# Conversions of a weight matrix spread over more blocks, a search begun later, and another search counted tile by tile

## The chip, the cores and the metric

The kernel runs on one core of a Trainium2 chip. The metric is the device time of one execution, in microseconds (us); the number given for a kernel is the median of its runs. The core has TensorE (PE; its weight loads are listed apart as PEld), VectorE (DVE), ScalarE (ACT), GpSimd (POOL) and SyncE (SP), which only starts transfers. Each engine works through its own queue in order, and so an instruction that waits holds up all that stands behind it on its engine.

## The reference

Three stages, all in float32. First attention over 4 batches of 8 heads with 576 rows and 64 columns a head, causal, with a bias from running sums of `s`. Its result, 2304 rows (tokens) of 512, goes to a layer of eight experts. Each token may go to one expert and each expert takes 288 tokens: all 2304 x 8 logits are sorted, and from the greatest down a token is given to an expert if it has none yet and the expert isn't full.

```python
order = np.argsort(-flat)
for idx in order:
    tok, e = (int(idx) // E, int(idx) % E)
    if assigned[tok] >= 0 or counts[e] >= cap:
        continue
    assigned[tok] = e
```

Each expert computes `relu(x @ w1[e]) @ w2[e]` with 1024 inner columns. The last stage is `(relu(x @ w_in) ** 2) @ w_out` with 2048 inner columns.

## The kernel before

**Attention first, then blocks.** The attention of all heads takes the first 230 us or so. The rest is `experts` (from line 945). Its matrix work is a list of 288 blocks, `order`, which I number from 0. A block is twelve matmuls (L1065 to L1067 through `mm3`, L1113 to L1115), since each product is made of three, high part by high part and the two mixed ones. A block has a kind: 1 and 2 are the first and second layer of an expert (288 columns a matmul), 3 and 4 are the third and fourth, `w_in` and `w_out`, for the tokens of two experts together (512 columns). Experts 0 and 1 have blocks 0 to 31 (kinds 1 and 2) and then 32 to 63 (kinds 3 and 4, mixed); experts 2 and 3 blocks 64 to 95 and 96 to 127; experts 4 and 5 blocks 128 to 159 and 160 to 191; expert 6 has 192 to 239, expert 7 has 240 to 287.

**The search.** The sort is replaced by eight searches (`route_phases`, L602), one for each place in the order in which experts fill up, place 0 to 7. A search needs the one before it. It finds the 288th largest key by six rounds of counting (two halves of three): VectorE compares all 20 tiles of keys with 42 thresholds (`compare`, L573, into the tile `wide`), TensorE counts the hits, VectorE turns the counts into flags, and TensorE broadcasts the result (L706, L715). The counts are made in one of two ways. For places below `GP` they are made tile by tile, 20 matmuls of 42 columns of weights (L684). For the others three tiles go together: 7 matmuls with 128 columns (L690), a copy to SBUF (L694), 3 selecting matmuls (L697). After the rounds come the position sums (L738, L739), four comparisons that make rows of slots (L763) with 2 x 10 matmuls (L770), and the list of indices (L774). With that list GpSimd gathers the expert's 288 rows from memory by three indirect transfers (L1023), and TensorE transposes them (`xt`; L1039 for expert 0, else L1032).

**How the search is spread.** `route_phases` is a generator; each `yield` ends a piece and gives a number for how long the piece's result takes: 1 for the keys and 1 for the best expert, in each round 2 after the comparison, 0.55 after the grouped count and 1 after the flags (in the tiled way 2 and 1), then 2, 1, 1, 1, 1. That is 29.3 for a grouped search. A counter, `wait[0]`, goes down by the cost of every block (1.0 for kinds 1 and 2; for kinds 3 and 4 1.7 with two experts or with expert 7, 0.9 with expert 6 alone). When it is at or under zero after a block, the next piece is emitted behind that block, and the counter goes up by the piece's number times a factor (`YS` = 0.5 for places 0 and 1, `YL` = 1.3 later; L1363). While fewer than two lists are done, a second look is taken in the middle of a block of kind 1 or 2 (`mid`, L1334). `RF` pieces of the search of place 1 are emitted before block 0, and then the transposes of expert 0's rows.

**What forces it.** Weights are loaded five blocks ahead (`LD`). When the loader reaches the first block of an expert it calls `need` (L1283), and this emits all pieces that are left until that expert's list is there, in one go, ahead of the block in hand. An expert that is the second of its pair is gathered at once and its transposes stand behind the last block of kind 1 of the expert before it (two of four) and the block after that (L1376); for the others the gathers are spread and the transposes follow some blocks later. For expert 1 the transposes stand behind blocks 12 and 13, for expert 3 behind 76 and 77, for expert 5 behind 140 and 141.

**The conversions.** `w_in` and `w_out` come as 64-bit floats and are converted piece by piece (`Convert`, L823), 32 pieces. The 16 of `w_out` are done in attention, two of `w_in` during the search of place 0, and 14 are left when block 0 begins. One `step` is: split a finished piece into high and low part (`store`; ScalarE, then GpSimd L993), finish a piece (`end`, VectorE L888), begin another (`begin` and `begin2`; ScalarE L862 and two VectorE operations, L877), and load one. Before, a step stands behind every second block (`CVM` = 2) from block 18 (`CV0`); and in the blocks of kind 3 of the first pair a loop takes care that the piece a block needs is there (L1082). VectorE also makes the low parts of many other splits (L993, L1143, L1160), squares for the third layer (L1179) and all of the search.

Of the kernel before, what the change touches and what calls it, by code (L numbers as in the profile page):

```python
# [471 lines left out]
NTOK, DM, E_, F1, F2 = 2304, 512, 8, 1024, 2048  # L472
# [3 lines left out]
KT, STEPS, GT = 42, (1681, 41, 1), 3  # L476
NG = (NT + GT - 1) // GT
F16, I16 = mybir.dt.float16, mybir.dt.int16
GP = 1
GY = 0.55  # L480
R0 = [0, 10, 15, 20]
RN = [0, 20]
# [119 lines left out]
def route_phases(tc, cn, L, rp, rps, eids, idxs):  # L602


    nc = tc.nc
# [15 lines left out]
    for ph in range(E_):  # L621
# [8 lines left out]
        else:  # L630
# [8 lines left out]
            khi, klo, wm, oh, cmp = fr.khi, fr.klo, fr.wm, fr.oh, fr.cmp  # L639
            key, base = khi, None  # L640
            for half in range(2):
                for n in range(3):
# [38 lines left out]
                    mi = rps.tile([128, 512], FT, name="mi")  # L681
                    if ph < GP:
                        for t in range(NT):
                            nc.tensor.matmul(mi[:KT, :8], cmp[:, KT * t:KT * t + KT], oh[:, t, :], start=t == 0,  # L684
                                             stop=t == NT - 1)
                    else:

                        for t in range(NG):
                            c0 = GT * KT * t
                            nc.tensor.matmul(mi[:, 128:128 + 8 * GT], cmp[:, c0:c0 + 128],  # L690
                                             oh[:, GT * t:GT * t + GT, :].rearrange("p t e -> p (t e)"), start=t == 0,
                                             stop=t == NG - 1)
                        ev = rp.tile([128, 8 * GT], F16, name="ev")
                        V.tensor_copy(ev, mi[:, 128:128 + 8 * GT])  # L694
                        yield GY
                        for t in range(GT):
                            nc.tensor.matmul(mi[:KT, :8], cn.sel[:, t, :], ev[:, 8 * t:8 * t + 8], start=t == 0,  # L697
                                             stop=t == GT - 1)
# [61 lines left out]
        n = NT // 4  # L760
# [28 lines left out]
NB1, NB2 = F1 // 128, F2 // 128  # L789
# [7 lines left out]
RS = 1  # L797
SD = 6
OD = 1
CVM = 2  # L800
XP = 4
XS = 'GGGS'
XN = [2, 2, 2, 2, 2, 3, 1, 2]
YS = 0.5
GD = 1
GS = 2
YL = 1.3
ML = 3
RF = 8
GE = 2  # L810
ME = 8
SL = 3
# [2 lines left out]
RB = 3  # L815
RL = 1
CVO = 0
CV0 = 18
WU = 10
TE = 8  # L820

# [123 lines left out]
def experts(tc, cn, L, xd, w1, w2, win, wout, out):  # L945
    nc = tc.nc
# [58 lines left out]
    def route_step():  # L1005
        l0 = len(idxs)
        y = next(route, 0)

        return y
# [59 lines left out]
    def block(blk, mid=lambda: None):  # L1069
# [9 lines left out]
            post.append((post1, (e, f, h)))  # L1079
        elif k == 3:  # L1080
            if e == 0:
                while conv.done < NB2 + f + 1:  # L1082
                    conv_step()
                conv.store(win_put)
            yh, yl = Y[e]
            n = 128 * len(GI[e])
            h = ps.tile([128, 512], FT, name="h", bufs=2)
            if len(CHUNKS[e]) == 2:

                o, yh, yl = h.rearrange("p (a n) -> p a n", a=2), *(  # L1090
                    y.rearrange("p d (a n) -> p d a n", a=2)[:, :, :, :256] for y in (yh, yl))
            else:
                o, yh, yl = h[:, :n], yh[:, :, :n], yl[:, :, :n]
            if f == 0 and len(CHUNKS[e]) == 2:

                for a in range(2):
                    for d in range(4):
                        mm3(o[:, a], winH[:, d, 0:128], winL[:, d, 0:128], yh[:, d, a], yl[:, d, a], d == 0, d == 3)
                post.append((post3, (e, f, h)))
                return  # L1100
            for d in range(4):
                mm3(o, winH[:, d, 128 * f:128 * f + 128], winL[:, d, 128 * f:128 * f + 128], yh[:, d], yl[:, d],
                    d == 0, d == 3)
            post.append((post3, (e, f, h)))
        elif k == 4:

            wh, wl = (w.rearrange("p c d -> p (c d)") for w in W.pop(blk))
            hi, lo = ST.pop((e, f))
            if f == 0:
                ACC[k, e] = [ps.tile([128, 512], FT, name=f"acc{g}") for g in range(len(GI[e]))]  # L1110
            for g, o in enumerate(ACC[k, e]):
                c0 = 128 * g
                T.matmul(o, hi[:, c0:c0 + 128], wh, start=f == 0, stop=False)  # L1113
                T.matmul(o, hi[:, c0:c0 + 128], wl, start=False, stop=False)  # L1114
                T.matmul(o, lo[:, c0:c0 + 128], wh, start=False, stop=f == NB2 - 1)  # L1115
            if f == NB2 - 1:
                post.append((post4, (e, ACC.pop((k, e)))))
        else:
            wh, wl = W.pop(blk)
            hi, lo = HT.pop((e, f))  # L1120
            last = NB1 - 1
            if f == 0:
                ACC[k, e] = [ps.tile([128, 512], FT, name=f"acc{d}") for d in range(4)]
            a = ACC[k, e]
            for d in range(4):
                mm3(a[d][:, :CAP], wh[:, d, :], wl[:, d, :], hi, lo, f == 0, f == last)
                if d == 1:
                    mid()
            if f == last:
                post.append((post2, (e, a)))  # L1130
# [209 lines left out]
    for n, blk in enumerate(order):  # L1340
# [19 lines left out]
        turn = blk[0] == 2 and blk[2] == NB1 - 1 and (blk[1] < TE or len(idxs) == E_)  # L1360
        if turn:
            flush()
        if len(idxs) < E_ and wait[0] <= 0 and n >= RS:  # L1363
            wait[0] += route_step() * (YL if len(idxs) > 1 else YS)
            routed = True
        flush()
        if conv.done < 2 * NB2 and n % CVM == CVO and n >= CV0:
# [66 lines left out]
```

## Time and profile before

| | us |
|---|---|
| median of 3 runs | 965.94 (963.07 to 967.32) |
| the profiled execution | 963.51 |
| its span, first to last instruction | 961.7 |
| PE busy | 898.0 (93%) |
| DVE busy | 575.1 (60%) |
| ACT busy | 455.8 (47%) |
| POOL busy | 405.7 (42%) |

The profile is of one execution. Busy time of PE is modelled, as matmuls are pipelined, and so pace is best read from the starts of matmuls. "Granted clock" is TensorE's clock as a share of 2.4 GHz; 0.50 is its lower level, 1.2 GHz. A bracket behind an instruction gives how long its engine was idle before it and what released it.

### The profile page before, as it was taken

To read this page: it belongs to the slowest core of one execution; us is meant where nothing else is said; L and a number is where in the kernel's file an instruction comes from. 1 tells how busy PE (TensorE), PEld (TensorE's weight loads), DVE (VectorE), ACT (ScalarE), POOL (GpSimd) and SP (SyncE) were. 2 spreads that over 40 slices of the span, in tenths; PEclk is the share of its full clock that TensorE was granted. 3 is DMA by queue.
4 is the path that set the end of the run, shared out by engine and by line. 5 is a ranking of instruction groups with operands and counts; after the bars stand their busy time and mean duration, and the time that the engine had idled before them with its cause. 6 is when DMAs were issued, how large, how long until landed. Compare 5 with 4: busy or idle time off the path is not lost.

```text
span 961.7 us, 16567 instructions
## 1 busy us (share of the span) xinstructions
PE 898.0 (93%) x5836; PEld 733.9 (76%) x5836; DVE 575.1 (60%) x1517; ACT 455.8 (47%) x1055; POOL 405.7 (42%) x330
## 2 busy tenths in 40 slices
PE   4999999998688798999999999989999999999996
PEld 3676767776478786777898777889888899898885
DVE  7787888887867988734756444756432344442222
ACT  6677767775334554233353233443432455553321
POOL 4454554443523656646442321633323454533233
PEclk9999999999589999999999999999999999999999
DMA  6877696733634632101641100455000160140001
GB/s 169 212 175 191 152 241 169 189 96 124 202 104 136 204 103 77 33 1 45 208 133 44 33 1 1 136 150 164 13 1 1 49 204 1 29 137 1 0 1 45
DMA packets 73971, 95.54 MB, mean 99 GB/s; under 512 B 8128, under 2 KB 53184, under 8 KB 73888
## 3 DMA queue, kind: packets, MB, share of 16 engines
q1 hardware_dynamic: 68560, 79.93, 30.4%
q0 software_dynamic: 3360, 11.01, 3.4%
q10 hardware_dynamic: 1968, 3.54, 1.0%
q8 instruction: 46, 0.75, 0.3%
q14 instruction: 37, 0.30, 0.1%
HBM read 80.31 MB, written 9.44 MB: 93 GB/s over the span
## 4 chain that ended last, share of the span: by engine, by line
PE 74%; DVE 14%; issue 4%; DMA 4%; POOL 2%; ACT 2%; SPq 0%; DVEq 0%; POOLq 0%; ACTq 0%
PE h L1065 10%; PE h L1067 9%; PE h L1066 9%; PE acc L1113 6%; PE acc L1114 6%; PE acc L1115 6%; PE av L271 5%; PE pt L244 5%; PE acc L1065 3%; PE acc L1067 3%; PE acc L1066 3%; PE sc L199 3%; DVE sg L877 2%; DVE Q L168 2%; PE sc L200 2%
## 5 line engine op out<-in xcount | busy, mean ns | idle before, releaser
L1180 POOL TENSOR_TENSOR sL<-s,sH 128x512 fp32r<-128x512 f32 (+1 forms) x80 | 111.6, 1394 | 252.0 <-DVE s L1179 245.3
L1175 ACT ACTIVATE s<-h 128x512 f32<-128x512 f32 (+1 forms) x80 | 44.5, 556 | 220.7 <-PE h L1067 220.6
L1179 DVE TENSOR_TENSOR s<-s 128x512 f32<-128x512 f32 (+1 forms) x80 | 53.3, 667 | 153.0 <-ACT sH L1178 152.8
L993 POOL TENSOR_TENSOR wL<-raw,wH 128x512 fp32r<-128x512 f32 x64 | 83.5, 1312 | 98.4 <-ACT wH L990 96.2
L1065 PE MATMUL h<-yH,winH 128*128 128x512 f32 (+1 forms) x332 | 124.1, 374 | 0.0
L1067 PE MATMUL h<-yH,winL 128*128 128x512 f32 (+1 forms) x332 | 121.2, 365 | 0.0
L1066 PE MATMUL h<-yL,winH 128*128 128x512 f32 (+1 forms) x332 | 121.0, 364 | 0.0
L1113 PE MATMUL acc<-wH,sH 128*128 128x512 f32 x288 | 116.3, 404 | 0.0
L990 ACT ACTIVATE wH<-raw 128x512 fp32r<-128x512 f32 x128 | 80.2, 629 | 76.0 <-DMA raw<-in_w 39.8
L1114 PE MATMUL acc<-wL,sH 128*128 128x512 f32 x288 | 113.5, 394 | 0.0
L1115 PE MATMUL acc<-wH,sL 128*128 128x512 f32 x288 | 113.5, 394 | 0.0
L227 ACT ACTIVATE e<-sc,nm 128x576 f32<-128x576 f32 (+4 forms) x160 | 84.1, 526 | 48.1 <-DVE junk L216 41.4
L216 DVE TENSOR_SCALAR_CACHE_REDUCE junk<-sc 128x576 bf16<-128x576 f32 (+4 forms) x160 | 77.6, 485 | 34.0 <-PE sc L202 25.7
L244 PE MATMUL pt<-ident,e 128*128 128x128 f32 x448 | 81.4, 288 | 5.3 <-ACT e L227 4.8
L199 PE MATMUL sc<-K,Q 128*128 128x288 f32 (+2 forms) x192 | 74.0, 390 | 10.5 <-DVE Q L152 10.5
L1065 PE MATMUL h<-xH,wH 128*128 128x288 f32 x256 | 81.0, 316 | 2.7 <-DVE hL L1143 2.7
L1065 PE MATMUL acc<-hH,wH 128*128 128x288 f32 x256 | 79.1, 309 | 0.0
L1066 PE MATMUL h<-xL,wH 128*128 128x288 f32 x256 | 77.0, 301 | 0.0
L1067 PE MATMUL h<-xH,wL 128*128 128x288 f32 x256 | 76.4, 299 | 0.1
L1067 PE MATMUL acc<-hH,wL 128*128 128x288 f32 x256 | 75.8, 296 | 0.0
L1066 PE MATMUL acc<-hL,wH 128*128 128x288 f32 x256 | 75.7, 296 | 0.0
L160 POOL TENSOR_TENSOR K<-k,K 64x1152 fp32r<-64x1152 f32 x15 | 39.7, 2648 | 78.8 <-DMA q<-in_qT 21.9
(225 smaller groups left out, 2107.4 us busy)
## 6 DMA issues: line engine op xcount, KB each, us to landing
raw<-in_w SPq DMA_DIRECT2D x128, 256.0 KB
k<-in_kT SPq DMA_DIRECT2D x30, 288.0 KB
q<-in_qT SPq DMA_DIRECT2D x30, 288.0 KB
r<-in_wout SPq DMA_DIRECT2D x16, 512.0 KB
r<-in_win SPq DMA_DIRECT2D x16, 512.0 KB
vb<-in_vm SPq DMA_DIRECT2D x16, 256.0 KB
Q<-Q SPq DMA_DIRECT2D x8, 288.0 KB
QB<-Q SPq DMA_DIRECT2D x7, 288.0 KB
```

Of the source, the lines that this page charges most:

```text
L199: nc.tensor.matmul(o, Q1[:, a, c0:c0 + 128], K1[:, a, x0:x1], start=True, stop=False)
L227: nc.scalar.activation(o, v, AF.Exp, bias=nm[:m], scale=0.125, accum_out=sums[b % 2][:m, i, hd % H:hd % H + 1])
L244: nc.tensor.transpose(pt[:, j, :m], (E4[hd % 2] if i == 4 else E[i])[:m, 128 * j:128 * j + 128], cn.ident[:m, :m])
L990: S.activation(hi, src, AF.Copy)
L993: (G if eng[1] == "G" else V).tensor_tensor(lo, src, f32(hi), op=OP.subtract)
L1065: T.matmul(o, wh, xh, start=first, stop=False)
L1066: T.matmul(o, wh, xl, start=False, stop=False)
L1067: T.matmul(o, wl, xh, start=False, stop=last)
L1113: T.matmul(o, hi[:, c0:c0 + 128], wh, start=f == 0, stop=False)
L1114: T.matmul(o, hi[:, c0:c0 + 128], wl, start=False, stop=False)
L1115: T.matmul(o, lo[:, c0:c0 + 128], wh, start=False, stop=f == NB2 - 1)
L1180: G.tensor_tensor(lo, s, f32(hi), op=OP.subtract)
```

## The change

Six edits. The matmuls that count tile by tile take 128 columns of weights instead of 42 (only the first 42 rows of the result are read), and the search of place 1 is now counted in that way too (`GP` = 2). `RF` goes from 8 to 3. Conversion steps stand behind every fourth block from block 8 instead of every second from block 18, and the loop in the third layer's blocks asks for one piece more than the block needs. The factor of the counter is now a list by the number of lists done (`YY`), read before the piece instead of after it; `mid` keeps `YS`. The search of place 2 isn't begun before block 20 (`R2`). And the counter isn't let below -1.0 when a piece is emitted.

```diff
-GP = 1
+GP = 2
...
-                            nc.tensor.matmul(mi[:KT, :8], cmp[:, KT * t:KT * t + KT], oh[:, t, :], start=t == 0,
+                            nc.tensor.matmul(mi[:, :8], cmp[:, KT * t:KT * t + 128], oh[:, t, :], start=t == 0,
                                              stop=t == NT - 1)
...
-CVM = 2
+CVM = 4
...
-YL = 1.3
+YY = [0, 0.45, 1.2, 1.0, 1.5, 1.5, 1.5, 1.5]
+R2 = 20
 ML = 3
-RF = 8
+RF = 3
...
-CV0 = 18
+CV0 = 8
...
-                while conv.done < NB2 + f + 1:
+                while conv.done < min(2 * NB2, NB2 + f + 2):
                     conv_step()
...
-        if len(idxs) < E_ and wait[0] <= 0 and n >= RS:
-            wait[0] += route_step() * (YL if len(idxs) > 1 else YS)
+        if len(idxs) < E_ and wait[0] <= 0 and n >= (R2 if len(idxs) == 2 else RS):
+            y = YY[len(idxs)]
+            wait[0] = max(wait[0], -1.0) + route_step() * y
```

## Rows read from the trace of the kernel before

**Rows 1.** The page: busy time, share and instructions of PE; its busy tenths in 40 slices of 24 us; the granted clock in the same slices.

```profile
PE 898.0 (93%) x5836; PEld 733.9 (76%) x5836; DVE 575.1 (60%) x1517; ACT 455.8 (47%) x1055; POOL 405.7 (42%) x330
...
PE   4999999998688798999999999989999999999996
...
PEclk9999999999589999999999999999999999999999
```

**Rows 2.** What PE waited for, over the whole span: us in total, times, longest.

```profile
PE mi L697 <- DVE ev L694: 8.3, 7, 3.5
PE mi L690 <- DVE wide L573: 7.6, 6, 2.6
...
PE mi L770 <- DVE wide L763: 4.4, 4, 2.3
...
PE mi L1032 <- DMA rows<-xd,idx: 1.4, 1, 1.4
```

**Rows 3.** Busy time of each engine between block borders: length, busy us (instructions) of PE, PEld, DVE, ACT, POOL, then granted clock, share of the DMA engines, GB/s.

```profile
269.50:289.20 19.70, 18.13 (x142) 15.64 (x142) 14.07 (x45) 7.92 (x17) 6.17 (x5) 0.96 0.37 109
289.20:306.20 17.00, 13.81 (x109) 12.96 (x107) 13.46 (x43) 5.50 (x12) 5.41 (x6) 0.90 0.47 139
306.20:346.50 40.30, 33.97 (x262) 32.14 (x260) 36.11 (x74) 23.41 (x46) 20.82 (x15) 0.96 0.56 169
346.50:397.30 50.80, 45.71 (x245) 35.27 (x245) 45.79 (x83) 23.25 (x41) 34.44 (x24) 1.00 0.23 69
397.30:451.30 54.00, 54.00 (x282) 40.41 (x278) 18.60 (x50) 17.85 (x33) 30.56 (x29) 1.00 0.07 20
```

**Rows 4.** The same columns for three stretches: blocks 192 to 200 and 174 to 185, with no search in between, and blocks 58 to 63, with a search step behind each.

```profile
766.00:780.40 14.40, 14.40 (x110) 14.37 (x109) 6.37 (x10) 7.00 (x14) 11.09 (x13) 1.00 0.76 230
715.70:749.30 33.60, 33.60 (x146) 27.11 (x145) 7.80 (x13) 10.53 (x18) 9.68 (x7) 1.00 0.00 1
...
432.60:451.30 18.70, 18.70 (x96) 13.90 (x96) 4.92 (x14) 6.49 (x11) 12.08 (x15) 1.00 0.11 29
```

**Rows 5.** The chain of waits from 250 to 275 us: start, us, what. The last tiled count of the search of place 0, its last broadcast and its index list; then a grouped count of the next search, its selection, and the transposes of expert 0's rows.

```profile
250.73 0.91 PE mi L684 x20
...
251.87 0.18 PE mi L715
...
257.52 0.16 DVE idx L774
...
266.01 0.38 PE mi L690 x7
...
266.65 0.24 PE mi L697 x3
266.89 2.13 PE acc L1039 x9
```

**Rows 6.** GpSimd's first and third gather for expert 0 (start, us, instruction), and, of all gathers, the time from issue to landing.

```profile
257.98 1.15 POOL L1023 DMA_INDIRECT rows<-xd,idx  x1 [2.11 <-DVE nt L780]
...
260.70 0.96 POOL L1023 DMA_INDIRECT rows<-xd,idx  x1 [0.30 <-issue]
...
DMA to landing us min/median/max: 3.3/3.9/4.7
```

**Rows 7.** The chain of waits from 295 to 304 us: expert 1's index list, the last of its gathers, and the transposes that waited for it.

```profile
295.80 0.17 DVE idx L774
...
298.78 4.68 DMA rows<-xd,idx
...
303.50 0.55 PE mi L1032 x3
```

**Rows 8.** VectorE's time on the conversions in two stretches: length, busy us (instructions), then the columns as before; first the two operations that begin a piece (L877), then the one that ends it (L888).

```profile
306.20:346.50 40.30, 10.64 (x14) 0.96 0.56 169
346.50:397.30 50.80, 16.15 (x12) 1.00 0.23 69
...
306.20:346.50 40.30, 6.95 (x7) 0.96 0.56 169
346.50:397.30 50.80, 5.89 (x7) 1.00 0.23 69
```

**Rows 9.** Weight loads of the tiled count (42 columns) and of the grouped count (128 columns): ns least, middle and most, first and last start, shape.

```profile
L684 PEld LDWEIGHTS <-wide x120: 97/123/131, 232.4 to 251.4; 128*42 128x42 bf16 x120
...
L690 PEld LDWEIGHTS <-wide x252: 95/96/118, 261.4 to 652.0; 128*128 128x128 bf16 x126
```

**Rows 10.** Three stretches of 2 us with PE's busy time and granted clock (columns as in group 3).

```profile
332.00:334.00 2.00, 0.00 (x0) 0.00 (x0) 2.00 (x2) 1.18 (x3) 2.00 (x2) 1.00 0.65 222
...
336.00:338.00 2.00, 2.00 (x9) 1.71 (x9) 1.93 (x7) 0.63 (x1) 0.00 (x0) 0.50 0.73 239
...
362.00:364.00 2.00, 0.04 (x2) 0.05 (x3) 1.94 (x4) 1.97 (x4) 1.45 (x2) 1.00 0.22 38
```

**Rows 11.** PE in order of time behind block 137, a count of the seventh search.

```profile
634.35 0.34 PE L690 MATMUL mi<-oh,wide 128*128 128x24 bf16 x7 [2.64 <-DVE wide L573]
```

**Rows 12.** Blocks 139 and 140 (columns as in group 3).

```profile
636.50:640.60 4.10, 4.10 (x33) 3.92 (x32) 3.11 (x9) 1.83 (x5) 0.00 (x0) 1.00 0.43 128
```

## Prediction

> **What bounds the kernel now.** I read the page first: TensorE is busy 898.0 of 961.7 us, and its slices fall below nine tenths at the start, from about 220 to 400 us and at the very end [rows 1]. Everything the change touches lies in the second place, so I cut the span at block borders (found by counting twelve matmuls to a block) [rows 3]. Blocks 0 to 13 last from 269.5 to 306.2, blocks 14 to 31 to 346.5, blocks 32 to 46 to 397.3, blocks 47 to 63 to 451.3. The pace with nothing in between is 14.4 us for nine blocks of the first two layers, 1.60 each, and 33.6 for twelve of the third and fourth, 2.80 each [rows 4]. A search step after a block costs TensorE about 0.32 more: six such blocks take 18.7, 3.12 each [rows 4]. A whole search is 21 such steps, 6.7 us.
>
> By that measure blocks 14 to 46 should take 18 x 1.60 + 15 x 2.80 + 6.7 = 77.5 us, and they take 91.1: 13.6 us of waiting. The reader is to see why in VectorE: 36.1 busy of 40.3 and 45.8 of 50.8, against 18.6 of 54.0 once the conversions are over [rows 3]. Seven conversions in each of the two stretches cost it (10.64 + 6.95)/7 = 2.5 and (16.15 + 5.89)/7 = 3.1 us apiece [rows 8]. The waits of TensorE name VectorE's results (the cast of the counts, the comparisons, the slot rows) and once the gathered rows [rows 2]. So here the bound is VectorE behind the search; from block 47 it is TensorE.
>
> **The change part by part.** I followed the planner's counter through the order of blocks, before and after. The searches of experts two to eight (places 1 to 7) run, before, in blocks 0-9, 10-42, 43-67, 68-99, 100-124, 125-155 and 156-162; after, in 0-10, 20-47, 48-73, 74-111, 112-139, 139-176, 177-182. The fourteen conversions left move from blocks 18, 20, ... 44 to 8, 12, ... 52 and two at 56. Against the own time of the profiled execution, 963.5 us (1.8 around the span):
>
> (a) Search of place 0, tile by tile with 128 columns: 20 matmuls in 0.91 us now [rows 5]. From tile 10 on a matmul also reads columns of the second comparison: 3 tiles later, three twentieths of 0.91, at most 0.14 a round, six rounds: +0.5, between -0.5 and +1.
>
> (b) Only three search steps before block 0. Now the transposes of the first rows start at 266.89, right behind a search matmul at 266.65 [rows 5]; the last gather was issued at 260.70 and lands 3.3 to 4.7 later [rows 6], 264.0 to 265.4, and transposes of the first two thirds can run before. Gain -3.0 (-1.4 to -3.5).
>
> (c) Blocks 0 to 8 take over the first two rounds. A tiled round is a count of 0.91 and a broadcast step, about 1.1; the grouped round is three steps, 0.96. Two more rounds +2.2, four dearer ones +0.6, less the cast's round trips, some 0.5 of waiting: +2.3 (0 to +4).
>
> (d) Blocks 9 to 13. After block 8 a conversion (2.5) now stands in VectorE's queue between the slot arithmetic and the slot comparisons, on which ten matmuls wait with one block, 1.6, as cover, as today: of its 2.5 I take 2.0 as added wait. The second pair of slot comparisons has half a block of cover: +0.5. The index list is then ready in the middle of block 10 instead of behind block 9, half a block, 0.8, later; from there to the landed rows it is 7.5 us now [rows 7], and the transposes behind block 12 wait for them in both. Sum +3.3 (+1 to +6). The rest of a moved step finds room: ScalarE is busy 5.5 of the 17.0 us there, GpSimd 5.4, the DMA engines half [rows 3]; its load on SP's queue stands between weight loads, but it fetches the third piece ahead, twelve blocks early, and without that cover would only delay a conversion that has none waiting on it until block 32.
>
> (e) Blocks 14 to 46: eight conversions instead of fourteen, six times about 2.8, 17 us of VectorE's 81.9 go. It stays loaded in blocks 20 to 31, where three conversions meet the new search's beginning; there I leave 3 us of waiting, and 1.3 in the longer blocks behind. Of 13.6 some 9.3 go: -9.3 (-13 to -6).
>
> (f) Blocks 47 to 63 take four conversions, 12 us more on VectorE's 18.6 of 54.0. Each lies under blocks of 2.80; the last parts of the weights are stored two blocks ahead of their use. +0.7 (0 to +3, one conversion of 3.1 in the open).
>
> (g) Expert 3's index list comes in block 73 instead of 67, its transposes stay at 76: 7.5 us against three blocks with steps, some 5, so a wait of up to 2.5; the scatter and gather bunched on GpSimd at 67 come apart, which gives some back: +0.7 (-1 to +3).
>
> (h) The sixth search is not done when block 139 needs expert 5's weights: 1.5 a unit, and a deficit cut at -1, stretch it past its 27 blocks. The loader forces six pieces at once, and in TensorE's queue they stand ahead of block 139. On GpSimd the gathers that follow find it idle (0.00 busy in those blocks now [rows 12]); on VectorE the low parts for the next weights queue behind the search, which TensorE doesn't feel while it stands. This chain has no cover. Its price: from the count to the broadcast about 1.2 (0.64 from count to selection [rows 5], as much again after); from the last broadcast to the index 251.87 to 257.52 plus 0.16, 5.8 [rows 5]; from there to the third gather's issue 3.0 (257.68 to 260.70), and 3.9 to landing [rows 6]: 13.9, then two sets of transposes, 0.5. Now the same blocks 139 and 140 take 4.1 [rows 12]. That is +10.3, less six search steps that today lengthen blocks 120 to 124 (-1.9), less today's wait of 2.64 at 634 behind the comparison, which the gather at block 131 brought about by holding GpSimd up [rows 11], plus a slower clock behind the gap: after a stretch with TensorE at 0.00 the granted clock is 0.50 (1.2 of 2.4 GHz) at 336 to 338, after one with 0.04 it stayed at 1.00 [rows 10]; I take 1.2. +7.0 (+4 to +11).
>
> Sum: 0.5 - 3.0 + 2.3 + 3.3 - 9.3 + 0.7 + 0.7 + 7.0 = +2.2, 965.7 against 963.5. The median shown is 965.94, 2.4 above the profiled execution, so I say 968.1.
>
> Here a rule speaks against (a) and (c). The rows: loading 128 columns of 16-bit weights takes 96 ns in the middle, 42 columns 123 [rows 9], so width costs nothing. The Trainium skill, TensorE: Matmul & The Clock Gate, section LDWEIGHTS, makes a load grow with its columns, 128/1.2 = 107 against 35 ns. By it the twelve tiled rounds would cost 12 x 20 x 72 ns = 17 us more, an estimate from that page; the trace does not agree.
>
> A second one bears on (e) and (f). A conversion's three VectorE operations cost 3.1 us where GpSimd is busy 34.4 of 50.8 and 2.5 where it is busy 20.8 of 40.3 [rows 3, 8]. The Trainium skill, SBUF — State Buffer, section Who interferes with whom, says that VectorE and GpSimd hold one port pair in turn for a whole instruction; the trace agrees in direction. By it the moved conversions get dearer in the longer blocks, towards the upper end of (f).
>
> **The rivals.** *Late rows decide (slower).* Three times the index list is finished so near its transposes that TensorE waits for rows: behind blocks 12, 76 and 140. For it: 7.5 us from index to rows and 1.43 of waiting now even with three blocks of cover [rows 2, 7]. Against it: the clock may be slow in the cover, which makes the cover longer. If landing takes 4.7 each time and VectorE delays the lists by a conversion, (d) is +6, (g) +3, (h) +11, together +9.0 over the forecast: 977. The forecast has 11.0 for the three; from some 14 on they decide.
>
> *VectorE was all of it (faster).* If relief takes nearly all waiting out of blocks 14 to 46, (e) is -13, and the forced chain finds GpSimd and VectorE empty, (h) +4, (d) +1: 9.0 under the forecast: 959. For it: blocks 47 to 63, with VectorE at a third, hold no such waits. Against it: VectorE keeps 65 us of work there.
>
> *Wide loads cost (slower).* A tiled count takes 0.91 us for 20 matmuls, 45 ns each [rows 5]; were that the load and grew from 42 columns to 128, it would be 139 ns, 1.9 us more a round and 22 in twelve rounds: 990. The load times [rows 9] speak against it; I give it 2 in 100.
>
> *It does less than it says:* conversions still bound blocks 20 to 31 and (e) is only -6, with (h) at +7: 971, at the border of slower.
>
> **How the numbers follow.** A measurement of this kernel can tell about 0.5%, 4.8 us, from no change. Chances: the forecast 0.44, late rows 0.24, VectorE alone 0.22, less than it says 0.08, wide loads 0.02. The forecast's own range is 962 to 973; the whole range, to keep 8 in 10, 956 to 979. Faster gets the third case and a little of the first, 0.24; slower late rows, wide loads, half of the fourth and part of the first, 0.34; the rest, 0.42, is no change.
>
> **What would show it.** Right: VectorE no longer nine tenths busy in blocks 32 to 46; blocks 14 to 46 in about 82 us; block 0 some 3 us nearer to the first gather; one stretch of 10 us or more with two gaps of TensorE about block 139, after which the clock is at its lower level; waits for rows behind blocks 12 and 76. Wrong: no gap at block 139, or blocks 14 to 46 still at 88 or more, or tiled counts much longer than 0.91.

## The result, and the profile after

The kernel after takes 977.80 us (median of 4 runs, 976.28 to 978.88) against 966.03 of the kernel before on the same chip: 1.0125 of it, 95% interval 1.0098 to 1.0152. It is slower by 11.8 us. The profiled execution of after took 976.28 us, its span is 974.5.

In rows of the kernel after, and of kernels made from it, line numbers from L808 on are one higher than in the kernel printed above.

The lines of the page that answer to [rows 1]:

```profile
PE 908.9 (93%) x5896; PEld 742.0 (76%) x5896; DVE 573.4 (59%) x1511; ACT 454.2 (47%) x1055; POOL 402.7 (41%) x330
...
PE   4999999998688899899899999979999999999996
...
PEclk9999999998597899999999999989999999999999
```

TensorE has 10.9 us more of busy time, though the change adds only 60 short matmuls. The third line says why: counted from zero, slices 9, 12, 13 and 26 (the last three are 292 to 341 and 633 to 658 us) have a lower granted clock than in [rows 1], and the same matmuls take longer there. TensorE's idle time (span less busy time) hardly grew, from 63.7 to 65.6 us.

What PE waited for, as in [rows 2]: us in total, times, longest.

```profile
PE mi L770 <- DVE wide L763: 8.7, 6, 3.8
PE mi L690 <- DVE wide L573: 7.9, 5, 3.8
PE mi L1033 <- DMA rows<-xd,idx: 7.3, 5, 3.0
...
PE mi L697 <- DVE ev L694: 0.3, 1, 0.3
```

One wait has gone, the cast of the counts (8.3 before). The comparisons kept theirs, the slot rows doubled theirs, and the late rows went from 1.4 to 7.3. So waits changed places more than they grew.

The stages, with the columns of [rows 3] and its borders from block 14 to 63 (blocks 0 to 8, 9 to 13, 14 to 31, 32 to 46, 47 to 63, 64 to 79, then 128 to 140 and 160 to 199):

```profile
264.40:287.70 23.30, 23.14 (x236) 20.88 (x237) 16.02 (x55) 8.49 (x18) 6.38 (x5) 0.85 0.38 109
287.70:308.80 21.10, 14.13 (x96) 13.41 (x95) 13.94 (x33) 7.14 (x15) 8.93 (x7) 0.77 0.53 157
308.80:346.50 37.70, 33.44 (x240) 31.91 (x238) 30.46 (x59) 19.27 (x40) 15.55 (x11) 0.90 0.52 152
346.50:397.00 50.50, 47.02 (x251) 35.56 (x250) 34.73 (x71) 21.39 (x38) 29.49 (x21) 1.00 0.15 46
397.00:455.20 58.20, 55.14 (x280) 41.42 (x278) 32.27 (x73) 20.88 (x37) 34.93 (x32) 0.97 0.14 40
...
615.80:649.60 33.80, 28.22 (x217) 26.21 (x216) 20.44 (x65) 10.97 (x22) 13.41 (x15) 0.90 0.54 164
683.90:791.90 108.00, 108.00 (x583) 87.74 (x582) 46.48 (x112) 38.96 (x71) 39.44 (x37) 1.00 0.16 47
```

VectorE is relieved as it was meant to be (34.7 of 50.5 us in blocks 32 to 46, where [rows 3] had 45.8 of 50.8), and the stage is no shorter. That is the puzzle of this case.

The table below cuts every profile of this study at the same blocks, by the first matmul of each; all later sections read from it. One profile per kernel, so the same code shows what such a cut is worth: after and x1 are the same up to block 75, and so are x9 and x10. Blocks 14 to 31 differ by 2.6 and 1.6 us in these pairs and blocks 47 to 63 by 1.6 and 0.0, while blocks 32 to 46 repeat within 0.05. x3 has no row, because its one profile was taken in a disturbed execution (1231.57 us), and the medians of x3 and x9 leave out one such run each.

```
kernel      start  0-8   9-13  14-31  32-46  47-63  64-79  80-127  128-140  141-159  160-199
before      269.5  21.7  15.0  40.4   50.8   54.0   34.5   127.0    27.8     33.8    104.4
after       264.4  23.3  21.1  37.8   50.4   58.3   35.2   125.4    33.8     34.3    108.0
x1          266.6  23.1  21.3  35.2   50.4   56.7   35.6   127.9    26.0     36.2    106.6
x2          265.8  23.1  17.4  38.7   51.1   53.8   36.4   125.4    33.6     34.3    108.0
x4          266.2  23.1  17.4  39.6   52.5   54.0   34.4   127.0    29.6     33.8    104.4
x5          264.6  23.3  21.9  35.5   48.7   54.5   34.7   125.4    33.7     34.3    108.0
x6          265.2  23.1  21.7  35.5   49.5   56.7   33.1   128.1    27.4     36.1    106.1
x7          270.5  21.7  14.9  40.6   51.4   53.6   36.4   127.0    28.9     33.8    104.4
x8          271.9  25.9  11.9  41.1   57.5   53.6   35.9   127.4    27.2     34.4    104.0
x9          265.9  23.1  17.2  37.3   48.6   56.9   36.5   125.4    34.0     34.3    108.0
x10         266.8  23.1  17.4  35.7   48.6   56.9   33.4   127.9    26.5     36.2    106.6
x11         265.8  21.2  14.6  35.7   50.8   59.3   33.7   127.6    28.1     36.1    106.2
x12         266.6  22.4  14.6  35.9   48.7   54.5   35.6   127.9    26.8     36.2    106.6
```

Three places of the trace of after show how the relief was lost. First, the wait at block 9: VectorE's conversion, the slot comparisons behind it, and TensorE's wait for them.

```profile
289.21 1.46 DVE L889 SCALAR_TENSOR_TENSOR ex<-ex,sg 128x512 int32<-128x512 int32 x1
290.71 1.74 DVE L878 TENSOR_SCALAR sg<-r 128x512 uint16<-128x512 uint16 x2
...
292.85 1.36 DVE L763 TENSOR_TENSOR wide<-r,iotah 128x640 bf16<-128x640 bf16 x3
...
293.39 0.69 PE L770 MATMUL mi<-vv,wide 128*128 128x6 bf16 x10 [3.85 <-DVE wide L763]
```

Here the conversion of block 8 (L889, L878) takes 3.2 us and stands between the slot arithmetic and L763.

Second, the wait at block 24, the first count of the third search. GpSimd and VectorE in order of time, then TensorE:

```profile
322.43 1.30 POOL L994 TENSOR_TENSOR winL<-ex,winH 128x512 fp32r<-128x512 f32 x1 [2.49 <-ACT winH L991]
323.97 1.29 POOL L994 TENSOR_TENSOR wL<-raw,wH 128x512 fp32r<-128x512 f32 x1 [0.24 <-PE h L1068]
328.25 1.42 POOL L994 TENSOR_TENSOR wL<-raw,wH 128x512 fp32r<-128x512 f32 x1 [2.98 <-ACT wH L991]
329.72 1.26 POOL L994 TENSOR_TENSOR winL<-ex,winH 128x512 fp32r<-128x512 f32 x1
```

```profile
322.52 1.39 DVE L544 TENSOR_TENSOR eq<-L,m 128x160 bf16<-128x160 f32 x1
...
324.03 1.27 DVE L547 TENSOR_TENSOR u<-u,m 128x20 int32<-128x20 int32 x1
...
325.59 0.67 DVE L889 SCALAR_TENSOR_TENSOR ex<-ex,sg 128x512 int32<-128x512 int32 x1
326.30 0.81 DVE L878 TENSOR_SCALAR sg<-r 128x512 uint16<-128x512 uint16 x2
...
328.46 1.25 DVE L560 TENSOR_SCALAR k2i<-khi 128x40 int16<-128x40 f32 x1
329.75 1.69 DVE L573 TENSOR_TENSOR wide<-thr,k2i 128x840 bf16<-128x840 bf16 x1
```

```profile
331.49 0.36 PE L690 MATMUL mi<-oh,wide 128*128 128x24 bf16 x7 [3.85 <-DVE wide L573]
```

The search began at 322.17, and the conversion of block 20 (L889, L878) stands between its first piece and its second. L544, L547, L560 and L573 each begin just behind the start of a GpSimd instruction and end 0.04 to 0.46 us behind its end; with none beside them L544 takes 0.33, L547 and L560 0.18 and L573 0.60. The first comparisons are ready 9.3 us after the search began, and TensorE had three blocks of 1.6 to fill that.

Third, the forced chain. TensorE and GpSimd in order of time, and the stretch with its granted clock:

```profile
637.90 0.18 PE L738 MATMUL mi<-prb,upper 128*128 128x40 bf16 x1 [1.29 <-DVE prb L729]
...
640.22 0.69 PE L770 MATMUL mi<-vv,wide 128*128 128x6 bf16 x10 [1.87 <-DVE wide L763]
...
648.08 0.33 PE L1033 MATMUL mi<-ident,rows 128*128 128x128 f32 x1 [0.43 <-DMA rows<-xd,idx]
649.24 0.66 PE L1033 MATMUL mi<-ident,rows 128*128 128x128 f32 x4 [0.84 <-DMA rows<-xd,idx]
```

```profile
642.27 0.98 POOL L1024 DMA_INDIRECT rows<-xd,idx  x1 [7.73 <-DVE nt L779]
...
644.82 0.95 POOL L1024 DMA_INDIRECT rows<-xd,idx  x1 [0.30 <-issue]
```

```profile
637.90:648.00 10.10, 7.38 (x47) 6.61 (x46) 6.60 (x26) 1.04 (x2) 2.89 (x3) 0.66 0.42 127
```

From the forced count at 635.23 to the last rows 14.0 us pass; blocks 138 to 140 take 16.0 us (8.0, 3.0, 5.0), where before they took 6.1. (Block 137, which held a wait before, went from 4.7 to 1.6.)

### The profile page after: what moved, and what is told of

Read it like the earlier page. It is cut to its first block, busy times and chain, and to the rows that moved or that the text cites. A ratio compares the mean times of both kernels' runs of the same rounds, so it can differ in the third digit from the quotient of the medians.

```text
span 974.5 us, 16679 instructions
## 1 busy us (share of the span) xinstructions
PE 908.9 (93%) x5896; PEld 742.0 (76%) x5896; DVE 573.4 (59%) x1511; ACT 454.2 (47%) x1055; POOL 402.7 (41%) x330
## 4 chain that ended last, share of the span: by engine, by line
PE 75%; DVE 13%; DMA 4%; issue 3%; ACT 2%; POOL 1%; SPq 0%; DVEq 0%; POOLq 0%; ACTq 0%
PE h L1066 10%; PE h L1067 9%; PE h L1068 9%; PE acc L1114 6%; PE acc L1115 6%; PE acc L1116 6%; PE av L271 5%; PE pt L244 5%; PE acc L1066 3%; PE acc L1067 3%; PE acc L1068 3%; PE sc L199 3%; DVE Q L168 2%; PE sc L200 2%; DMA rows<-xd,idx 2%
## 5 line engine op out<-in xcount | busy, mean ns | idle before, releaser
L1180 DVE TENSOR_TENSOR s<-s 128x512 f32<-128x512 f32 (+1 forms) x80 | 51.1, 638 | 135.7 <-ACT sH L1179 135.4
L1066 PE MATMUL acc<-hH,wH 128*128 128x288 f32 x256 | 81.5, 318 | 0.0
L1067 PE MATMUL acc<-hL,wH 128*128 128x288 f32 x256 | 77.9, 304 | 0.0
L1068 PE MATMUL acc<-hH,wL 128*128 128x288 f32 x256 | 77.9, 304 | 0.0
```

The costliest lines, as they stand in the source:

```text
L1066: T.matmul(o, wh, xh, start=first, stop=False)
L1067: T.matmul(o, wh, xl, start=False, stop=False)
L1068: T.matmul(o, wl, xh, start=False, stop=last)
```

## The experiments

All were timed beside the kernel before on the same chip; the ratios are to it, with the 95% interval. Five kernels take the change apart first: x1 and x2 take a part away from after, x3, x4 and x7 add a part to before.

**x1, the later searches counted as before.**

```
-YY = [0, 0.45, 1.2, 1.0, 1.5, 1.5, 1.5, 1.5]
+YY = [0, 0.45, 1.2, 1.0, 1.3, 1.3, 1.3, 1.3]
```

> The kernel after with the fifth to eighth search counted at 1.3 a unit as in the kernel before, so that the sixth search ends in block 133 and nothing is forced in front of block 139. Theory (the forced chain has no cover and costs its own time): blocks 138 to 140 lose their 10 us of gaps, six search steps come back into blocks 128 to 133 (+1.9), and the kernel takes about 970.5 against 977.8. Rival (the rows of expert 5 or 6 would be waited for in any case, or the steps of the last searches cost the same somewhere else): no better than 975.

Measured 972.72, ratio 1.0075 (1.0053 to 1.0096): 0.5% less than after. Blocks 128 to 140 fall from 33.8 to 26.0, blocks 80 to 127 and 141 to 159 take the steps back (+2.5, +1.9), blocks 160 to 199 give 1.4 back. The forced chain cost its own time; it fell 2 short of the theory's 970.5 and clear of the rival.

**x2, the conversions where they were before.**

```
-CVM = 4
+CVM = 2
...
-CV0 = 8
+CV0 = 18
...
-while conv.done < min(2 * NB2, NB2 + f + 2):
+while conv.done < NB2 + f + 1:
```

> The kernel after with the conversions where the kernel before has them (every second block from 18 to 44). Theory (spreading relieves VectorE by a few us in blocks 14 to 46, and gives most of it back in front of the slot rows at block 9 and in blocks 47 to 63): blocks 0 to 13 some 2 us shorter, blocks 14 to 46 some 5 longer, blocks 47 to 63 some 4 shorter, together 977, the same within 1.5. Rival 1 (the relief is real and the rest of the loss is the searches' order): 981 or more. Rival 2 (the spread conversions themselves are the loss): 972 or less.

Measured 971.58, 1.0066 (1.0043 to 1.0088), 0.6% less than after: the second rival. Blocks 9 to 13 get 3.7 us shorter and blocks 47 to 63 4.5, while blocks 14 to 46 get only 1.6 longer. In the new order of the searches the spread conversions are a loss.

**x3, the spread conversions alone on the kernel before.** The edit of x2 the other way round.

> The kernel before with the conversions alone spread (every fourth block from 8, stored one block earlier). By the steps of the prediction (blocks 9 to 13 +2, blocks 14 to 46 -9.3, blocks 47 to 63 +0.7): 959.5 against 966.0. Theory after the result (a conversion put in front of a search's operation costs a stall wherever it is put, so waits only move): 965, blocks 14 to 46 between 86 and 90 us and blocks 47 to 63 some 3 longer.

Measured 964.00, 0.9988 (0.9969 to 1.0006): no difference that can be told, as the theory after the result had it, and not the 6.5 us that the prediction's steps give. How its stages moved is not known, as it has no row in the table.

**x4, the second search alone tile by tile.**

```
-GP = 1
+GP = 2
...
-nc.tensor.matmul(mi[:KT, :8], cmp[:, KT * t:KT * t + KT], oh[:, t, :], start=t == 0,
+nc.tensor.matmul(mi[:, :8], cmp[:, KT * t:KT * t + 128], oh[:, t, :], start=t == 0,
...
-RF = 8
+RF = 3
```

> The kernel before with the second search alone counted tile by tile, in 128 columns, and three search steps in place of eight ahead of block 0; its list is then ready in block 10 instead of 9. Theory (the start comes 5 us nearer, blocks 0 to 8 give 1.6 back, the later list about 1): 963.5 against 966.0. Rival (the later list and its late rows take the gain): 966 or more. Wide loads at their price by columns would give 988.

Measured 963.18, 0.9980 (0.9959 to 1.0001). The start comes 3.3 us earlier, blocks 0 to 8 cost 1.4, and blocks 9 to 13 cost 2.4 (blocks 12 and 13 3.8, less 1.4 in blocks 9 and 10). This is the theory's time, and nothing like 988.

**x7, the late third search alone on the kernel before.**

```
-if len(idxs) < E_ and wait[0] <= 0 and n >= RS:
+if len(idxs) < E_ and wait[0] <= 0 and n >= (20 if len(idxs) == 2 else RS):
```

> The kernel before with the third search alone begun at block 20 instead of 10. Theory (the search's beginning is cut short: its first comparisons have one block of cover behind the conversions at 20 and 22, and TensorE waits some 4 us at block 24; its list in block 69 instead of 67 brings a wait for rows of about 1 at 76; blocks 14 to 20 gain 2 to 3): 968. Rival (blocks 10 to 20 without a search give all of it back or more): 965 or less.

Measured 969.11, 1.0049 (1.0034 to 1.0064): slower, as expected, but only partly in the places expected. Block 23 lasted 7.6 us in its profile, yet blocks 14 to 31 together are as long as before (40.6 and 40.4); blocks 64 to 79 cost 1.9, and 32 to 46 and 128 to 140 0.7 and 1.0.

Added up, the four parts come close to the whole: tile by tile -0.20%, late begin +0.49%, spreading in the new order +0.59 (after less x2), the count +0.50 (after less x1), together +1.38 against +1.25 measured.

**x6, after with the third search begun at once and counted as before.**

```
-YY = [0, 0.45, 1.2, 1.0, 1.5, 1.5, 1.5, 1.5]
-R2 = 20
+YY = [0, 0.45, 1.3, 1.3, 1.3, 1.3, 1.3, 1.3]
+R2 = 1
```

> The kernel after with the third search begun at once (block 10 instead of 20) and the third to eighth counted at 1.3 as before: the second search tile by tile and the spread conversions stay. Theory (the late begin costs the gap at block 24 and the wait for rows at 76, and the count the forced chain): those three go, some 3.5 at block 9 stay: 967. Rival (the late begin itself relieves blocks 14 to 20 and its loss is only a shift): 972 or more.

Measured 968.70, 1.0041 (1.0014 to 1.0068), between the two and nearer to the theory. It differs from x4 by the spread conversions and small changes of the count, and is 0.6% slower. In the profiles the relief is plain to see and is given back on both sides of it: blocks 14 to 46 take 85.0 instead of x4's 92.1, blocks 9 to 13 4.3 more and blocks 47 to 63 2.6 more. So the loss by spreading doesn't hang on the late begin. Its size is seen in the medians alone: the profiled executions of x4 and x6 took the same, 966.7 and 966.6.

**x5, the same conversions two blocks later.** This is the test of the puzzle: not fewer conversions, only other places.

```
-CVO = 0
-CV0 = 8
+CVO = 2
+CV0 = 10
```

> The kernel after with the same conversions, one every fourth block, but two blocks later each (10, 14, 18, ... instead of 8, 12, 16, ...), so that none stands ahead of the slot comparisons of blocks 9 and 45 or between the third search's beginning (blocks 20 to 22) and its first count at 24. Theory (what counts is where a conversion stands in VectorE's queue, not how many there are): blocks 9 to 14 fall from 21 to 18, the gap of some 4 us at block 24 goes, blocks 46 and 47 lose 2; 969 to 971 against 977.8. Rival (the number of conversions beside a busy GpSimd is what costs, wherever they stand): 975 or more.

Measured 971.23, 1.0070 (1.0051 to 1.0090), 0.55% less than after. The total is near the theory's, but not all of its parts are. Blocks 32 to 46 get 1.8 us shorter and blocks 47 to 63 3.8, the latter although VectorE does more there than in after:

```profile
287.90:309.80 21.90, 14.37 (x96) 13.17 (x95) 11.45 (x30) 5.96 (x13) 7.38 (x6) 0.77 0.41 126
345.20:393.90 48.70, 46.65 (x250) 35.66 (x250) 31.15 (x68) 18.58 (x34) 27.79 (x20) 1.00 0.14 44
393.90:448.30 54.40, 53.34 (x281) 40.47 (x278) 36.66 (x76) 23.69 (x42) 37.72 (x33) 1.00 0.17 49
```

In the last row VectorE is busy 36.7 us and the stage takes 54.4; in after it was 32.3 and 58.2. Load does not set this stage, position does. Block by block, after is longer at 35, 38, 46, 47, 51 and 54 (by 0.6 to 2.4), x5 at 36, 44 and 56 (by 0.7 to 1.5), and the others agree. The largest are 46 and 54. TensorE waits there in after as follows, and what it waits for at 54 is VectorE's comparison:

```profile
396.42 0.68 PE L770 MATMUL mi<-vv,wide 128*128 128x6 bf16 x10 [1.93 <-DVE wide L763]
...
425.20 0.34 PE L690 MATMUL mi<-oh,wide 128*128 128x24 bf16 x7 [1.83 <-DVE wide L573]
```

```profile
421.79 3.35 DVE L573 TENSOR_TENSOR wide<-thr,k2i 128x840 bf16<-128x840 bf16 x1
```

Ahead of both stands a conversion (of blocks 44 and 52) in VectorE's queue, and L573 took 3.35 instead of 0.60 beside GpSimd. x1, the same code there, repeats blocks 46, 51 and 54 within 0.02 us; block 47 it does not (3.2 instead of 4.7), as its clock did not fall behind block 46.

Two parts missed. The gap at block 24 did not go: blocks 24 and 25 take 7.5 us here, 9.2 in after, 7.1 in x1, and 9.2 in x2, where the conversions lie as before, so it comes with the late begin. And blocks 9 to 13 did not fall to 18: they take 21.9. The conversion of block 10 no longer delays VectorE's list, and hits another queue. VectorE's list and GpSimd behind it in x5:

```profile
293.51 0.17 DVE L774 TENSOR_REDUCE idx<-mi 128x3 int32<-128x6 f32 x1 [0.47 <-PE mi L770]
```

```profile
296.17 1.65 POOL L994 TENSOR_TENSOR winL<-ex,winH 128x512 fp32r<-128x512 f32 x1 [5.86 <-ACT winH L991]
297.96 0.99 POOL L1024 DMA_INDIRECT rows<-xd,idx  x1
```

GpSimd stood idle for 5.86 us in front of the conversion's low part, whose input wasn't there yet, and the gathers, whose list was ready at 293.7, had to stand behind it until 297.96. TensorE then waited 5.9 us for the rows.

**x8, tile by tile with eight steps ahead of block 0.** The edit of x4 without the line RF.

> The kernel before with the second search counted tile by tile and still eight steps ahead of block 0, so that its list is ready in block 6. Theory (the gain at the start goes, some 3, but the wait for rows at blocks 12 and 13, 3.8 with three steps, goes as well, and eight cheaper steps are in the open): 963, as with three steps. Rival (the start decides): 966 or more.

Measured 970.72, 1.0056 (1.0038 to 1.0075): a miss. The rows are no longer late (blocks 9 to 13: 11.9), but the start is 2.4 us later and blocks 0 to 8 4.2 longer than before, and, as a surprise, blocks 32 to 46 take 57.5, at a granted clock of 0.88. (The profiled execution, 975.24 us, was the longest of the seven.) With the list four blocks earlier than in x4, the searches behind it fall on other conversions. VectorE and GpSimd there:

```profile
387.09 2.98 DVE L544 TENSOR_TENSOR eq<-L,m 128x160 bf16<-128x160 f32 x1
...
395.43 3.13 DVE L560 TENSOR_SCALAR k2i<-khi 128x40 int16<-128x40 f32 x1
```

```profile
386.36 0.97 POOL L1023 DMA_INDIRECT rows<-xd,idx  x1 [0.15 <-issue]
387.34 1.29 POOL L993 TENSOR_TENSOR wL<-woutR,wH 128x512 fp32r<-128x512 f32 x1
388.57 1.30 POOL L993 TENSOR_TENSOR winL<-ex,winH 128x512 fp32r<-128x512 f32 x1
...
395.02 0.97 POOL L1023 DMA_INDIRECT rows<-xd,idx  x1
396.00 1.29 POOL L993 TENSOR_TENSOR wL<-woutR,wH 128x512 fp32r<-128x512 f32 x1
397.24 1.26 POOL L993 TENSOR_TENSOR winL<-ex,winH 128x512 fp32r<-128x512 f32 x1
```

Each of the two small VectorE operations began during a gather and lasted until the two GpSimd instructions right behind it were over, 3 us.

**x9 and x10, conversions from block 14 on; in x10 also the count of x1.**

```
-CVO = 0
-CV0 = 8
+CVO = 2
+CV0 = 14
```

> The kernel after with conversions every fourth block from 14 (14, 18, 22, ...), none in blocks 8 to 12. Theory (at block 8 a conversion stands in VectorE's queue ahead of the slot comparisons, at block 10 its low part stands in GpSimd's queue ahead of the gathers; either way the rows come 3 to 4 us late, and without one blocks 9 to 13 take the 17.4 that they take without spread conversions; the later stages stay as with the shift by two blocks): 967 against 971.2 with the shift alone. Rival (the later list of the tiled search is what makes the rows late, whatever stands in the queues; the conversion left out costs again further on): 970 or more.

> As the run with conversions from block 14, and the fifth to eighth search counted at 1.3 a unit, so that nothing is forced at block 139. Theory (the two repairs add, since they lie 300 us apart: -4.5 and -5): 962, faster than before by 3. Rival (the repaired start makes the clock or a wait later give some back): 966 or more.

Measured 969.03, 1.0037 (1.0016 to 1.0059), and 965.53, 1.0005 (0.9985 to 1.0025). Blocks 9 to 13 do fall to 17.2 and 17.4, as expected, but the total of x9 lies between the theory's and the rival's, nearer to the rival's: the conversion left out at the front comes back as a second one at block 50, and blocks 47 to 63 take 56.9 instead of 54.5. By the ratios to before, x9 takes off 0.88%, x1 0.50% and x10 1.20%, so within the intervals the two repairs add; x10's 965.5 is 3.5 over the 962 expected.

**x11, the lists earlier.** On top of x10:

```
-R2 = 20
-RF = 3
+R2 = 16
+RF = 4
```

> As the run before it in this list, and the lists earlier: four search steps instead of three ahead of block 0 (second list in block 9 instead of 10) and the third search begun at block 16 instead of 20, in the same place to the conversions (expert 3's list in block 71 instead of 73). Theory (the waits for rows at blocks 12 and 76 shrink by 1.6 and 3, the fourth step costs 1 at the start): 3 less, 959. Rival (the waits for rows are fed by the slow clock and do not shrink, or the start gives all back): the same 962 or more.

Measured 963.65, 0.9981 (0.9966 to 0.9997): the rival's time. The fourth step costs nothing that shows (start 265.8, blocks 0 to 8 21.2) and blocks 9 to 13 get 2.8 shorter: together 5.7 us in the profiles. The other half missed: blocks 64 to 79 are no shorter, and with the third search elsewhere in its relation to the doubled conversions, blocks 52 and 53 take 4.6 us more than before, blocks 47 to 63 59.3.

**x12, the conversion of block 10 behind the gathers.**

```
-YY = [0, 0.45, 1.2, 1.0, 1.5, 1.5, 1.5, 1.5]
-RF = 3
-CVO = 0
-CV0 = 8
+YY = [0, 0.45, 1.2, 1.0, 1.3, 1.3, 1.3, 1.3]
+RF = 4
+CVO = 2
+CV0 = 10
```

> The kernel after with four search steps ahead of block 0, conversions in blocks 10, 14, 18, ... and the fifth to eighth search counted at 1.3; the third search begins at block 20 as in the kernel after. The second list is ready in block 9 and its gathers are issued there, so the same conversion at block 10 that cost 4.5 us with three steps now stands behind them on GpSimd. Theory (position in the queues decides): blocks 9 to 14 take 15 as in the run with earlier lists, blocks 32 to 47 and 47 to 64 the 48.7 and 54.5 of the run with the shift by two blocks, blocks 128 to 141 the 26 of the run counted at 1.3; sum of the best stages 7 under the kernel before: 958.5. Rival (any conversion in blocks 8 to 12 makes the rows late, and what one stage gains the clock takes in the next): 963 or more.

Measured 959.47, 0.9940 (0.9919 to 0.9961): faster than before by 5.5 us and than after by 18. GpSimd at the same place as in x5:

```profile
293.83 0.96 POOL L1024 DMA_INDIRECT rows<-xd,idx  x1 [2.33 <-DVE nt L779]
...
297.49 1.65 POOL L994 TENSOR_TENSOR winL<-ex,winH 128x512 fp32r<-128x512 f32 x1 [0.16 <-ACT winH L991]
```

The list is ready at 293.55 (in x5 at 293.7), the gathers go out 4.1 us earlier, and the same low part follows them. Blocks 9 to 13 take 14.6, with 0.8 us of waiting for rows where x5 had 5.9. This is as much as in x11, which has no conversion there: behind the gathers the conversion costs nothing, where with three steps it cost 4.5 (x5 21.9, x10 17.4).

## Why the prediction was right or wrong

The forecast was 968.1, +2.2 over the kernel before; measured were +11.8, 977.8, inside the range of 956 to 979 but on the side that had a chance of 0.34. That the range held owes much to its width: (e), (f) and steps left out behind block 160 missed by 6.4, 3.6 and 3.7 us, all to the same side.

The loss was paid mostly at the lower clock. In the profiled executions TensorE's busy time grew by 10.9 us and its idle time by 1.9. Over all runs the granted clock was 0.972 in the mean in before (29 runs, timed beside x9) and 0.964 in after (4 runs); with the share that is missing, times the run, that is at most 27 and 36 us lost to it, 9 of the 11.8 us. The prediction had 1.2 us for the clock, in (h) alone. Waits come ahead of the falls: each of the six stretches at 0.50 between blocks 9 and 199 of after lies at or behind a wait named in this text, at blocks 9, 12, 24, 46, 76 and 138.

By the table, step by step in the two profiled executions, 963.51 and 976.28:

- (a), (b), the start: -2.5 forecast, -5.1 in the table. Two profiles with the start of before (before, x7) and eight with that of after give means of 270.0 and 265.7, -4.3. From the first gather to block 0, where (b) lies, it is 11.5 us in the two and 7.4 to 7.9 in the eight. Right in kind, too small: eight of the twelve transposes ran before the last rows had landed. By the prediction's own rows the earlier start (1.5 to 2.9) and two thirds of the transposes' 2.13 make a gain of 2.9 to 4.3, where it took 1.4 to 3.5.
- (c) blocks 0 to 8: +2.3 forecast, +1.6 (1.4 in nearly all others). Right, but its price of a count was not, nor that of (a): the 0.91 was read at a granted clock of 0.50 (250.0 to 251.7 us of before). In these blocks a count of 128 columns took 0.66 at 1.00, and at 0.50 the last one of place 0 took 0.69 in after. The loads of 128 columns took 98 ns in the mean here (120 of them in these blocks), so *Wide loads cost* is out. The 35 ns that the rule of the Trainium skill, TensorE: Matmul & The Clock Gate, section LDWEIGHTS, makes for 42 columns, an estimate, is not what [rows 9] show, and a time by columns is not what x4 shows.
- (d) blocks 9 to 13: +3.3 forecast, +6.1, the upper bound. The mechanism is right, both terms were too small: x2 and x4 put the later list at 2.4 instead of 0.8, because half a block of lateness became a longer wait for rows (3.2 us instead of 1.4), and the conversion at 3.7 instead of 2.5.
- (e) blocks 14 to 46: -9.3 forecast, -2.9: **the step that failed.** It took VectorE's load as the whole cause of the waits. VectorE was relieved by 16.7 us in these blocks, and TensorE by far less. By the table, spreading is worth 6.6 there with the early begin (before 91.1 and x4 92.1, against x6 85.0) and 4.1 with the late one (x7 92.0 and x2 89.8, against after 88.2 and x1 85.5). The 3 us left for blocks 20 to 31 did not hold the late begin's gap at block 24, 3.85 and a slower clock behind it, and the 1.3 left for the longer blocks did not hold what stands ahead of the search's operations there: with the conversions two blocks later blocks 32 to 46 are 1.8 shorter, and blocks 14 to 46 take 84.1 to 86.0 (x5, x9, x10, x12).
- (f) blocks 47 to 63: +0.7 forecast, +4.3 (+2.7 in x1, where the clock stayed up at block 47): this failed too, by position: VectorE's work rose by 13.7 us, 12 were forecast. "Each lies under blocks of 2.80" counted cover, and not what stands behind in the queue. Two blocks later the term is +0.5.
- (g) blocks 64 to 79: +0.7 forecast, +0.7. The wait for rows at block 76 was 3.0 in two parts, beyond the 2.5, and other waits went.
- (h) blocks 80 to 159: +7.0 forecast, +4.8. Of it, six steps that leave blocks 120 to 124 were -1.9; blocks 80 to 127 gave -1.6. The rest, +8.9, stands against +6.4 in blocks 128 to 159. The chain itself was forecast at 13.9 to landing and took 14.0. Right in place and kind; the 1.2 for a slower clock behind the gap did not come, as the clock was at 0.66 inside the chain and back at 1.00 from 648 us on. x1 takes the chain away.
- Blocks 160 to 199: nothing forecast, +3.7. (h) subtracted the steps that leave blocks 120 to 124 and **left out that later searches are pushed back in turn**: TensorE begins 15 steps of the last two searches in these blocks where it began 2 before, 3.7/13 = 0.28 us each.

The rival *Late rows decide* named the measured time almost exactly (977) and was wrong about the cause: it had (d) right at +6, but rows cost 7.3 us in all, 5.9 more than before, and x1, x2 and x5 each win about as much without making all rows timely. *VectorE was all of it* falls with x5, where blocks 47 to 63 take less time with more work on VectorE. *It does less than it says* had (e)'s failure in kind, at half its size and without (f). By the prediction's own signs, VectorE below nine tenths, the gaps at 139, the waits for rows behind 12 and 76 and the nearer block 0 all came; the lower clock behind block 139 did not, and blocks 14 to 46 at 88.2 were the sign named as wrong.

What stays open: why spreading costs nothing in the old order (x3) and 0.6% in the new one (x2, x6), since x3 has no stages to read.

## What to carry to other kernels

Before pricing a relief by the busy share of an engine, look for the two or three operations that another engine waits for, and ask what will stand ahead of them in every in-order queue that they pass, here VectorE's for the comparisons and GpSimd's for the gathers. Moving background work by two blocks, at the same amount, was worth 5 us or more; with the gathers put ahead of it and the count taken back (x12) the slower change became the faster kernel. When steps leave one stage, add them where they arrive. And price a wait with the clock that may fall behind it: at block 47 the same code took 3.2 us in x1 and 4.7 in after.

## What was not expected of the hardware

A VectorE operation of 0.18 us lasted 3.13 us while two GpSimd instructions ran one after the other (x8), and 1.25 beside one (after). In the blocks of all thirteen profiles L544, L547 and L560 took 0.17 to 0.34 us whenever no tensor-tensor of GpSimd ran beside them (145 of 145). The five that lasted about 3 us (one each in before, x4 and x6, two in x8) all began during a gather with two tensor-tensors right behind it. The rule of the Trainium skill, SBUF — State Buffer, section Who interferes with whom, that the two engines hold a shared port pair one at a time, for a whole instruction, agrees in kind; the trace adds that a short operation can wait out a second instruction too.

The granted clock after the same wait differed between two executions of the same code. At block 46 TensorE waited 1.93 us in after and in x1, and was busy 0.48 and 0.47 us of the 2.4 up to the end of the wait. In after the clock then stood at 0.50, 1.2 of 2.4 GHz, from 398.0 to 401.4 us (the last column but two):

```profile
394.00:396.40 2.40, 0.48 (x3) 0.04 (x1) 2.37 (x6) 1.75 (x3) 1.49 (x2) 1.00 0.28 62
...
398.00:401.40 3.40, 3.40 (x10) 2.29 (x9) 0.23 (x1) 0.00 (x0) 2.50 (x2) 0.50 0.70 197
```

In x1 it stayed at 1.00 at the same place:

```profile
395.99 0.68 PE L770 MATMUL mi<-vv,wide 128*128 128x6 bf16 x10 [1.93 <-DVE wide L763]
```

```profile
393.60:396.00 2.40, 0.47 (x3) 0.04 (x2) 2.37 (x6) 1.75 (x3) 1.47 (x2) 1.00 0.30 82
...
397.60:401.00 3.40, 3.40 (x25) 2.62 (x24) 1.26 (x6) 0.00 (x0) 2.52 (x2) 1.00 0.68 196
```

At block 24 the two differ already in the wait, 3.85 us in one piece in after, with a clock of 0.50 behind it, and 0.69 and 2.29 in x1, with 1.00: L547, L560 and L573 met no GpSimd instruction in x1 and took 0.18, 0.17 and 0.60 us, where in after they took 1.27, 1.25 and 1.69.
